# One request of weights moved up, one reciprocal moved ahead, one copy split over two engines: the start of an attention and GLU kernel on Trainium2

## The chip, the cores and the metric

The kernel runs on one core of one Trainium2 chip. The metric is the device time of one execution in microseconds (us). One execution was also recorded by the hardware profiler; all starts below are counted from the beginning of that record's span.

The engines are named as the profile names them: PE is TensorE (matmuls and transposes; PEld are its weight loads), DVE is VectorE, ACT is ScalarE, POOL is GpSimd, and SP is SyncE, which here only issues transfers.

## The reference

The input x has 2048 rows of 512 bf16 numbers. With `xn = layernorm(x)` over each row, the output is

```
q, k, v = split(xn @ wqkv)                 # 32 heads of 16
s = softmax(q . k[t - 2w], w = 0..7) v @ wo   # 8 keys, every second row back
g = silu((gelu(xn @ w_gate) * (xn @ w_up)) @ w_down)   # inner width 1792
out = x + s * g
```

So every projection needs the normalized rows first, with the 512 features on the partitions, that is, transposed.

## The kernel before

The rows are cut into 16 tiles of 128 (`NT`), and four tiles make one of four blocks (`TPQ` tiles, `TQ` = 512 rows, `NJ` blocks). For each block the kernel computes q, k and v (`qkv`), the gate and up projections (`glu`), the attention in pieces that are placed between those by a table written by hand (`at` and `run`, L426 to L468), and the down projection with the output (`down`, `finish`). The order of the program is the order on each engine: the schedule is manual (L51), and nothing reorders it later. Waits between engines are put in by the framework where one instruction reads or overwrites what another writes.

What the change touches is the start, up to the first 10 us, and it is all in the first block.

- **Loads** (L95 to L105). `load_x` (L84) fetches n tiles of x in one request, `load_w` (L90) a range of columns of a weight matrix. All are issued by SP, in the order written: x tiles 0, 1, 2, the q columns of `wqkv` (512 KB), x tile 3, the k columns, the v columns, x tiles 4 to 7, and then the gate and up weights and the other tiles.
- **Statistics of the first four tiles** (L171 to L180). `first_moments(t)` computes the row statistics (`bn_stats`, L172) and their aggregate (`bn_aggr`, L173) on VectorE, and the square root of the variance on ScalarE (L174). `first_normalize(t)` takes the reciprocal on VectorE (L179) and then normalizes (`normalize`, L194), which gives the tile `xn`.
- **Transposes** (L199 to L214). `transpose(t)` makes four 128 by 128 transposes on TensorE (L203) into one PSUM tile `tr`, and copies that into `xnT`, in one or in several parts; the copies run on ScalarE (L212), or on VectorE where `copy` is given (L214).
- **Warming matmuls** (`warm_up`, L216) on constants fill TensorE's time until the first tile is ready.
- **q, k and v of block 0** (L488 to L508). The first two tiles (`HQ` = 256 rows) are projected ahead of the other two. Their four q blocks go into one PSUM tile of four banks, `q4` (L488), in two rounds over the contraction. Each k block is one PSUM tile `qkv_ps` (L253), four matmuls (L238), and is drained to SBUF by ScalarE (L256 for q, L259 for k). Between them stand the transposes of tiles 2 and 3 (L495, L499), with their copies on VectorE. Then come the second 256 rows, and v.
- **PSUM.** Warming matmuls, transposes, projections and most outputs share the pool `mm` with four buffers (L71), which are given out in turn: a new tile takes the buffer of the tile four allocations earlier.

ScalarE's order in the start is: square roots of tiles 0 and 1, the copies of the transposes of tiles 0 and 1, square roots of tiles 2 and 3, four q drains, four k drains. VectorE's is: statistics and aggregate of tile 0, of tile 1, reciprocal and normalize of tile 0, of tile 1, statistics of tiles 2 and 3, their normalizes, the copies of their transposes.

Of the kernel before, what the change touches and what calls it, by code (L numbers as in the profile page):

```python
# [28 lines left out]
def kernel(  # L29
# [13 lines left out]
    nc = tc.nc  # L43
    B, S, D = A_x.shape
    DF = B_w_gate.shape[1]
    NT, NC, NF, NJ = S // P, D // P, DF // P, S // TQ
    TPQ = TQ // P
# [27 lines left out]
    x_sb = big.tile([P, NT, D], BF16, name="x_sb")  # L75
# [8 lines left out]
    def load_x(t, n=1):  # L84
        nc.sync.dma_start(
            out=x_sb[:, t : t + n, :],
            in_=x2d[t * P : (t + n) * P, :].rearrange("(t p) d -> p t d", p=P),
        )

    def load_w(dst, src, lo, hi):  # L90
        nc.sync.dma_start(
            out=dst[:, :, lo:hi], in_=src.rearrange("(k p) n -> p k n", p=P)[:, :, lo:hi]
        )

    for t in range(TPQ - 1):  # L95
        load_x(t)
    load_w(wqkv_sb, A_wqkv, 0, D)
    load_x(TPQ - 1)
    for i in range(1, 3):
        load_w(wqkv_sb, A_wqkv, i * D, (i + 1) * D)  # L100
    load_x(TPQ, TPQ)
# [5 lines left out]
    def load_late_weights():  # L107
# [16 lines left out]
        out=vT.rearrange("(k p) n -> p k n", p=P)[:, :, 0:PAD],  # L124
        in_=zpad[:],
# [32 lines left out]
    stats = const.tile([P, NT, nc.vector.BN_STATS_DIM], F32, name="stats")  # L158
# [9 lines left out]

    nc.scalar.activation(out=std[:, 0, :], in_=epsc[:], func=AF.Sqrt, bias=epsc[:], scale=1.0)

    def first_moments(t):  # L171
        nc.vector.bn_stats(out=stats[:, t, :], in_=x_sb[:, t, :])  # L172
        nc.vector.bn_aggr(out=mv[:, t, :], in_=stats[:, t, :])  # L173
        nc.scalar.activation(  # L174
            out=std[:, t, :], in_=mv[:, t, 1:2], func=AF.Sqrt, bias=epsc[:], scale=1.0
        )

    def first_normalize(t):
        nc.vector.reciprocal(out=rstd[:, t, :], in_=std[:, t, :])  # L179
        normalize(t)  # L180

    def moments(t):
        nc.vector.bn_stats(out=stats[:, t, :], in_=x_sb[:, t, :])
# [8 lines left out]
    def normalize(t):  # L192
        xn = xns[t] = xnp.tile([P, D], BF16, name="xn")
        nc.vector.tensor_scalar(  # L194
            out=xn[:], in0=x_sb[:, t, :], scalar1=mv[:, t, 0:1], scalar2=rstd[:, t, :],
            op0=ALU.subtract, op1=ALU.mult,
        )

    def transpose(t, parts=1, copy=None):  # L199
        xn = xns[t]  # L200
        tr = mm.tile([P, NC * P], BF16, name="tr", tag="mm")
        for c in range(NC):
            nc.tensor.transpose(tr[:, c * P : (c + 1) * P], xn[:, c * P : (c + 1) * P], ident[:])  # L203
        j, i = divmod(t, TPQ)
        if i == 0:
            xnT[j] = xtp.tile([P, NC, TQ], BF16, name="xnT")
        dst = xnT[j][:, :, i * P : (i + 1) * P]
        src = tr[:].rearrange("p (c n) -> p c n", c=NC)
        for k in range(parts):
            c = slice(k * NC // parts, (k + 1) * NC // parts)  # L210
            if copy is None:
                nc.scalar.activation(out=dst[:, c], in_=src[:, c], func=AF.Copy)  # L212
            else:
                copy(out=dst[:, c], in_=src[:, c])  # L214

    def warm_up(n, cols):  # L216

        ps = mm.tile([P, TQ], F32, name="warm_ps", tag="mm")
        for _ in range(n):
            nc.tensor.matmul(  # L220
                ps[:, 0:cols], lhsT=nc.const_aps.tensor(1.0, [P, P], BF16),
                rhs=nc.const_aps.tensor(1.0, [P, cols], BF16), start=True, stop=True,
            )
# [24 lines left out]
    def qkv(j, fo, i0=0, n=TQ, ps=None):  # L248
        which, c = divmod(fo, NC)
        if fo == 0 and i0 == 0:  # L250
            st[j]["q"] = qp.tile([P, NC, TQ], BF16, name="q_sb")
        if ps is None:
            ps = mm.tile([P, n], F32, name="qkv_ps", tag="mm")[:]  # L253
            project(ps, wqkv_sb, fo * P, j, i0, n)
        if which == 0:
            nc.scalar.activation(out=st[j]["q"][:, c, i0 : i0 + n], in_=ps, func=AF.Copy)  # L256
        elif which == 1:
            lo = PAD + j * TQ + i0
            nc.scalar.activation(out=k_sb[:, c, lo : lo + n], in_=ps, func=AF.Copy)  # L259
        else:  # L260
            vst = sm4.tile([P, TQ], BF16, name="vst")
            nc.scalar.activation(out=vst[:], in_=ps, func=AF.Copy)  # L262
            lo = PAD + j * TQ
            nc.sync.dma_start(out=vT[c * P : (c + 1) * P, lo : lo + TQ], in_=vst[:])
# [168 lines left out]
    for i in range(TPQ):  # L433
        at(("qkv", 0, i), normalize, TPQ + i)
        at(("glu", 0, 7 + i), moments, 2 * TPQ + i)
        if i < 2:
            at(("glu", 0, i), transpose, TPQ + i)
        at(("glu", 0, 8 + i), normalize, 2 * TPQ + i)
        at(("glu", 1, 0), transpose_by_dma, 2 * TPQ + i)
        at(("glu", 1, 10 + i), moments, 3 * TPQ + i)  # L440
        at(("qkv", 2, 2 * i), normalize, 3 * TPQ + i)
        at(("glu", 2, 0), transpose_by_dma, 3 * TPQ + i)
# [28 lines left out]
    HT = TPQ // 2  # L471
    HQ = HT * P
    warm_up(18, TQ // 2)
    warm_up(4, P)
    first_moments(0)
    first_moments(1)
    first_normalize(0)
    transpose(0)
    first_normalize(1)
    warm_up(4, P)  # L480
    transpose(1, parts=2)
    warm_up(4, P)
    first_moments(2)
    first_moments(3)
    first_normalize(2)
    first_normalize(3)

    q4 = att.tile([P, NC, TQ], F32, name="q4_ps", tag="quad")  # L488
    qs = [q4[:, fo, 0:HQ] for fo in range(NC)]
# [2 lines left out]
            project(qs[fo], wqkv_sb, fo * P, 0, 0, HQ, dks)  # L492
    for fo in range(NC):
        qkv(0, fo, 0, HQ, qs[fo])
    transpose(HT, copy=nc.vector.tensor_copy)  # L495
    for fo in range(NC, 2 * NC):
        qkv(0, fo, 0, HQ)
        if fo == NC:
            transpose(HT + 1, copy=nc.vector.tensor_copy)  # L499
    for t in range(TPQ, 2 * TPQ):  # L500
        moments(t)
    sum_constants()
# [61 lines left out]
```

The softmax here doesn't subtract the row's maximum and nothing guards it: scores larger than these inputs give would overflow.

## Time and profile before

| what | value |
|---|---|
| median of 4 runs | 229.87 us (229.72 to 230.38) |
| the profiled execution | 229.62 us |
| its span | 227.9 us |
| TensorE busy | 221.6 us, 97% |
| VectorE busy | 147.7 us, 65% |
| ScalarE busy | 129.7 us, 57% |
| granted TensorE clock | 1.00 |
| first q matmul | 6.64 us |
| DMA from 9.4 to 17.7 us | 369 GB/s |

The span is what the profiler recorded between the first and the last instruction; the device time is 1.7 us longer. A line of a timeline begins with the start and the length in us, then the engine, the line of the kernel and the operation, then output and inputs by name, their shapes, and how many such instructions were put together. The length of such a group reaches from the first start to the last end. In square brackets stands how long the engine had been idle, and who released it.

### The profile page before, as it was taken

The numbers are of one execution on the slowest core, as the hardware profiler recorded it, in microseconds if no ns is written. First come the engines' busy times: TensorE is split into PE (matmuls) and PEld (weight loads), VectorE is DVE, ScalarE is ACT, GpSimd is POOL, SyncE is SP. The second block draws the span as 40 slices with busy tenths as digits, with TensorE's granted clock in tenths as the row PEclk, the third lists the DMA queues.
The fourth block names the chain that finished last, engine by engine and source line by source line (L and its number), as shares of the span: only waits on it lengthen the run. The fifth ranks groups of instructions, "written<-read, shape, count | busy, mean of one in ns | idle before, by whom it ended". The sixth has DMA issues, their size and how long they took to land.

```text
span 227.9 us, 3495 instructions
## 1 busy us (share of the span) xinstructions
PE 221.6 (97%) x1300; PEld 106.1 (47%) x1320; DVE 147.7 (65%) x234; ACT 129.7 (57%) x213; POOL 12.8 (6%) x44
## 2 busy tenths in 40 slices
PE   7999999999999999999999999999999999999993
PEld 5864444444444444444444444444444444444453
DVE  4694996899596298865945369735476429943324
ACT  3779769764423876467621686746642387647210
POOL 1055023100000000110000000000000000000000
PEclk9999999999999999999999999999999999999999
DMA  5999589991399211110287511110139700001011
GB/s 164 361 371 373 142 165 198 214 238 42 97 196 211 65 27 26 26 29 0 92 168 168 140 30 23 26 36 5 40 106 213 175 26 3 0 6 26 0 45 48
DMA packets 31264, 24.62 MB, mean 108 GB/s; under 512 B 10896, under 2 KB 31248, under 8 KB 31248
## 3 DMA queue, kind: packets, MB, share of 16 engines
q1 hardware_dynamic: 31248, 24.41, 43.3%
q8 instruction: 10, 0.16, 0.3%
q14 instruction: 6, 0.05, 0.1%
HBM read 18.74 MB, written 4.34 MB: 101 GB/s over the span
## 4 chain that ended last, share of the span: by engine, by line
PE 93%; ACT 3%; DVE 1%; DMA 1%; issue 1%; ACTq 0%; DVEq 0%
PE u_ps L238 21%; PE y_ps L394 21%; PE g_ps L238 19%; PE qkv_ps L238 17%; PE s_ps L410 6%; PE L_ps L295 3%; PE o_ps L357 3%; DMA x_sb<-in_A_x_dram 1%; PE q_ps L238 1%; ACT u L384 1%; ACT xnT L212 1%; DVE stats L172 1%; ACT L382 1%; PE den_ps L315 0%; PE tr L203 0%
## 5 line engine op out<-in xcount | busy, mean ns | idle before, releaser
L238 PE MATMUL u_ps<-xnT,wu_sb 128*128 128x512 bf16 x224 | 57.5, 379 | 0.3
L238 PE MATMUL g_ps<-xnT,wg_sb 128*128 128x512 bf16 x213 | 56.3, 379 | 0.4
L394 PE MATMUL y_ps<-wd_sb,h 128*128 128x512 bf16 (+1 forms) x236 | 50.2, 366 | 0.1
L386 DVE TENSOR_TENSOR h<-ge,u 128x512 bf16<-128x512 bf16 x56 | 23.8, 424 | 37.6 <-ACT u L384 37.2
L284 DVE TENSOR_TENSOR pk<-q_sb,k_sb 128x2048 bf16<-128x2048 bf16 x32 | 37.5, 1218 | 7.0 <-ACT k_sb L259 7.0
L382 ACT ACTIVATE ge<-g_ps 128x512 bf16<-128x512 f32 x56 | 33.5, 598 | 14.9 <-PE g_ps L238 13.8
L384 ACT ACTIVATE u<-u_ps 128x512 bf16<-128x512 f32 x56 | 33.5, 598 | 14.7 <-PE u_ps L238 14.7
L238 PE MATMUL qkv_ps<-xnT,wqkv_sb 128*128 128x512 bf16 (+1 forms) x203 | 40.5, 354 | 0.3
L343 DVE TENSOR_TENSOR pv<-E,v_arr 128x2048 bf16<-128x2048 bf16 x32 | 38.7, 1220 | 0.7 <-PE u_ps L238 0.6
L394 PEld LDWEIGHTS <-h 128*128 128x128 bf16 x238 | 23.3, 98 | 25.3
L238 PEld LDWEIGHTS <-wu_sb 128*128 128x128 bf16 x224 | 21.9, 98 | 26.7 <-issue 0.3
L238 PEld LDWEIGHTS <-wg_sb 128*128 128x128 bf16 x224 | 21.2, 98 | 27.3 <-issue 3.0
L402 ACT ACTIVATE sl<-y_ps 128x512 bf16<-128x512 f32 (+1 forms) x17 | 9.7, 572 | 41.4 <-PE y_ps L394 39.0
L238 PEld LDWEIGHTS <-wqkv_sb 128*128 128x128 bf16 x224 | 21.8, 98 | 19.6 <-issue 0.2
L418 DVE TENSOR_TENSOR m<-s_ps,sl 128x512 bf16<-128x512 f32 (+1 forms) x17 | 11.2, 658 | 22.3 <-PE s_ps L410 22.3
L410 PE MATMUL s_ps<-wo_sb,oT 128*128 128x512 bf16 (+1 forms) x66 | 15.8, 366 | 0.2
L262 ACT ACTIVATE vst<-qkv_ps 128x512 bf16<-128x512 f32 x16 | 9.6, 597 | 6.7 <-PE qkv_ps L238 6.7
L188 POOL TENSOR_TENSOR rstd<-rstd,mhalf 128x1 f32<-128x1 f32 x12 | 7.7, 640 | 87.3 <-DVE rstd L185 87.3
L259 ACT ACTIVATE k_sb<-qkv_ps 128x512 bf16<-128x512 f32 (+1 forms) x20 | 10.2, 516 | 3.5 <-PE qkv_ps L238 3.2
L369 DVE TENSOR_TENSOR oT<-o_ps,rb 128x1024 bf16<-128x1024 f32 x8 | 9.4, 1218 | 2.5 <-DMA rb<-rs_d 2.5
L256 ACT ACTIVATE q_sb<-qkv_ps 128x512 bf16<-128x512 f32 (+1 forms) x16 | 8.7, 544 | 3.2 <-PE qkv_ps L238 3.0
L410 PEld LDWEIGHTS <-oT 128*128 128x128 bf16 x68 | 6.7, 98 | 7.2
(46 smaller groups left out, 104.0 us busy)
## 6 DMA issues: line engine op xcount, KB each, us to landing
v_arr<-vT SPq DMA_DIRECT2D x16, 520.0 KB, 5.5
vT<-vst SPq DMA_DIRECT2D x16, 128.0 KB, 1.9
out_dram<-o_t SPq DMA_DIRECT2D x15, 128.0 KB, 1.9
wg_sb<-in_B_w_gate_dram SPq DMA_DIRECT2D x2, 896.0 KB, 10.9
wu_sb<-in_B_w_up_dram SPq DMA_DIRECT2D x2, 896.0 KB, 12.9
wd_sb<-in_B_w_down_dram SPq DMA_DIRECT2D x1, 1792.0 KB, 12.5
wqkv_sb<-in_A_wqkv_dram SPq DMA_DIRECT2D x3, 512.0 KB, 5.0
x_sb<-in_A_x_dram SPq DMA_DIRECT2D x3, 512.0 KB, 11.9
```

Source lines behind the costliest of these rows:

```text
L238: nc.tensor.matmul(ps, lhsT=w[:, dk, lo : lo + P], rhs=xnT[j][:, dk, i0 : i0 + n], start=(dk == 0), stop=(dk == NC - 1),)
L259: nc.scalar.activation(out=k_sb[:, c, lo : lo + n], in_=ps, func=AF.Copy)
L262: nc.scalar.activation(out=vst[:], in_=ps, func=AF.Copy)
L284: nc.vector.tensor_tensor(out=pk[:], in0=st[j]["q"][:], in1=k_sb[:, :, off : off + TQ], op=ALU.mult)
L343: nc.vector.tensor_tensor(out=pv[:], in0=st[j]["E"][:, wh, :].unsqueeze(1).to_broadcast([P, 4, TQ]), in1=st[j]["va"][:, 4 * g : 4 * g + 4, ...
L382: nc.scalar.activation(out=ge[:], in_=g_ps[:], func=AF.Gelu_apprx_tanh)
L384: nc.scalar.activation(out=u[:], in_=u_ps[:], func=AF.Copy)
L386: nc.vector.tensor_tensor(out=h[:], in0=ge[:], in1=u[:], op=ALU.mult)
L394: nc.tensor.matmul(y[:], lhsT=st[j][fc][:, tt * P : (tt + 1) * P], rhs=wd_sb[:, fc, cols], start=(fc == 0), stop=(fc == NF - 1),)
L402: nc.scalar.activation(out=sl[:], in_=y[:], func=AF.Silu)
L410: nc.tensor.matmul(s[:], lhsT=st[j]["oT"][:, g, tt * P : (tt + 1) * P], rhs=wo_sb[:, g, cols], start=(g == 0), stop=(g == NC - 1),)
L418: nc.vector.tensor_tensor(out=m[:], in0=s[:], in1=sl[:], op=ALU.mult)
```

## The change

It has four parts, all in the start.

1. The request for the q columns of `wqkv` goes from behind x tile 2 to behind x tile 1; x tiles 2 and 3 follow it together.
2. The pieces of `first_moments` and `first_normalize` are cut anew into `first_stats`, `first_moments` and `first_rstd`, so that tile 0's reciprocal stands between tile 1's statistics and tile 1's aggregate on VectorE. For tiles 2 and 3 the order stays as it was: statistics and aggregate of one and of the other, then reciprocal and normalize of each.
3. Of the two halves of the copy of tile 1's transpose, the first goes to VectorE and the second stays on ScalarE. On VectorE it stands ahead of the statistics of tile 2.
4. The transposes of tiles 2 and 3 go from ahead of the first and the second k block to behind the first and the second k block.

```diff
-    for t in range(TPQ - 1):
-        load_x(t)
+    load_x(0)
+    load_x(1)
     load_w(wqkv_sb, A_wqkv, 0, D)
-    load_x(TPQ - 1)
+    load_x(2)
+    load_x(3)
...
+    def first_stats(t):
+        nc.vector.bn_stats(out=stats[:, t, :], in_=x_sb[:, t, :])
+
     def first_moments(t):
-        nc.vector.bn_stats(out=stats[:, t, :], in_=x_sb[:, t, :])
         nc.vector.bn_aggr(out=mv[:, t, :], in_=stats[:, t, :])
...
-    def first_normalize(t):
+    def first_rstd(t):
         nc.vector.reciprocal(out=rstd[:, t, :], in_=std[:, t, :])
-        normalize(t)
...
-            if copy is None:
+            if copy is None or k % 2:
                 nc.scalar.activation(out=dst[:, c], in_=src[:, c], func=AF.Copy)
...
+    first_stats(0)
     first_moments(0)
+    first_stats(1)
+    first_rstd(0)
     first_moments(1)
-    first_normalize(0)
+    normalize(0)
     transpose(0)
-    first_normalize(1)
+    first_rstd(1)
+    normalize(1)
     warm_up(4, P)
-    transpose(1, parts=2)
+    transpose(1, parts=2, copy=nc.vector.tensor_copy)
     warm_up(4, P)
-    first_moments(2)
-    first_moments(3)
-    first_normalize(2)
-    first_normalize(3)
+    for t in (2, 3):
+        first_stats(t)
+        first_moments(t)
+    for t in (2, 3):
+        first_rstd(t)
+        normalize(t)
...
-    transpose(HT, copy=nc.vector.tensor_copy)
     for fo in range(NC, 2 * NC):
         qkv(0, fo, 0, HQ)
-        if fo == NC:
-            transpose(HT + 1, copy=nc.vector.tensor_copy)
+        if fo < NC + 2:
+            transpose(HT + fo - NC, copy=nc.vector.tensor_copy)
```

## The prediction

> **What bounds the kernel now.** I read four views in this order: the page, the busy time by stretches, the timelines of VectorE and ScalarE over the start, and that of TensorE. The page first:
>
> ```profile
> PE 221.6 (97%) x1300; PEld 106.1 (47%) x1320; DVE 147.7 (65%) x234; ACT 129.7 (57%) x213; POOL 12.8 (6%) x44
> PE 93%; ACT 3%; DVE 1%; DMA 1%; issue 1%; ACTq 0%; DVEq 0%
> ```
>
> TensorE is busy for 97% of the span and holds 93% of the chain that ended last, at a granted clock of 1.00. From 20.8 to 220 us it is busy 198.2 of 199.2 us (the stretches), and it computes the same list of matmuls after the change. So the change can only move time in the start: whatever TensorE begins earlier or later there is carried to the end, plus any new gap. The start runs on VectorE and ScalarE until about 6.6 us:
>
> ```profile
> 4.51 0.18 DVE L173 BATCH_NORM_AGGREGATE mv<-stats 128x2 f32<-128x6 f32 x1
> 4.61 0.13 DVE L179 RECIPROCAL rstd<-std 128x1 f32<-128x1 f32 x1
> 4.78 0.41 DVE L194 TENSOR_SCALAR xn<-x_sb,mv,rstd 128x512 bf16<-128x512 bf16 x1
> 5.11 0.16 DVE L179 RECIPROCAL rstd<-std 128x1 f32<-128x1 f32 x1
> 5.30 0.41 DVE L194 TENSOR_SCALAR xn<-x_sb,mv,rstd 128x512 bf16<-128x512 bf16 x1
> 5.63 0.69 DVE L172 BATCH_NORM_STATS2 stats<-x_sb 128x6 f32<-128x512 bf16 x1
> ...
> 6.77 0.69 DVE L172 BATCH_NORM_STATS2 stats<-x_sb 128x6 f32<-128x512 bf16 x1 [0.24 <-DMA x_sb<-in_A_x_dram]
> ```
>
> Tile 0's reciprocal starts 0.10 us behind tile 1's aggregate; its input, the square root on ScalarE, was there at 4.29 (4.00 + 0.29). Tile 2's statistics start at 5.63, tile 3's wait for their data until 6.77. Then the first real matmuls, and who drains them:
>
> ```profile
> 5.77 0.40 PE L203 MATMUL tr<-ident,xn 128*128 128x128 bf16 x4
> 6.01 0.39 PE L220 MATMUL warm_ps<-const-bfloat16-1.0 128*128 128x128 bf16 x4
> 6.64 1.91 PE L238 MATMUL q_ps<-xnT,wqkv_sb 128*128 128x256 bf16 x16 [0.24 <-ACT xnT L212]
> 8.39 0.39 PE L203 MATMUL tr<-ident,xn 128*128 128x128 bf16 x4
> 8.61 0.60 PE L238 MATMUL qkv_ps<-xnT,wqkv_sb 128*128 128x256 bf16 x4
> 9.05 0.39 PE L203 MATMUL tr<-ident,xn 128*128 128x128 bf16 x4
> ...
> 8.59 1.21 ACT L256 ACTIVATE q_sb<-q_ps 128x256 bf16<-128x256 f32 x4 [0.58 <-PE q_ps L238]
> 9.66 1.50 ACT L259 ACTIVATE k_sb<-qkv_ps 128x256 bf16<-128x256 f32 x4
> ```
>
> The first q matmul, at 6.64, waits for ScalarE's copy of the first half of tile 1's transpose (that copy starts at 6.21 and ends near 6.60). ScalarE begins to drain q at 8.59, only when the last of the 16 q matmuls has ended (6.64 + 1.91 = 8.55), and drains the first k block from 9.66 to 10.07. TensorE's and ScalarE's timelines at 20 us show a rule of this kernel's PSUM pool of four buffers that decides the case:
>
> ```profile
> 20.12 0.60 ACT L382 ACTIVATE ge<-g_ps 128x512 bf16<-128x512 f32 x1
> 20.77 1.02 PE L238 MATMUL u_ps<-xnT,wu_sb 128*128 128x512 bf16 x4
> ```
>
> The allocations run tr, g, u, tr, g, u here; the second u is the fifth after the first g, takes its buffer, and starts 0.05 us after that g was drained (20.12 + 0.60 = 20.72). So a block waits until the block four allocations before it is drained.
>
> [...]the trace has 0.42 for that copy (8.81 and 9.47). [...]landings follow issues: q 6.4, x tile 3 6.74, k 8.2, v 9.8 us.
>
> **The change part by part.**
>
> *Requests.* q's weights are issued third instead of fourth: at about 1.70 instead of 2.18, as the x requests before it take 0.39 to 0.43 us of SP's queue each. Between 3.6 and 4.6 us the DMA engines moved only 92 to 195 GB/s, so the half megabyte starts into a gap: it lands about 0.48 us earlier, near 5.9. Tile 2 now stands behind it. A tile is 0.35 us (128 KB at about 370 GB/s). All together starts 0.48 earlier and tile 2's 0.35 comes behind, so k lands 0.13 earlier, near 8.1, tile 3 near 6.6, tile 2 near 6.26; at worst, with no gain from the gap, tile 2 lands 0.35 ahead of today's tile 3, at 6.39. SP's later requests keep place and time. On the path q's weights are worth nothing, since ScalarE's copy (6.60) ended after their landing (6.4); but without the earlier landing an earlier copy would be worth little.
>
> *Reciprocal ahead of the aggregate.* Tile 1's statistics run from 3.82 to 4.48. The reciprocal goes at about 4.40 (instructions without a wait start some 0.08 us before the end of the one before: 5.63 against 5.71), the aggregate stays at 4.51, and the normalize follows at 4.61 instead of 4.78: 0.17 us for tile 0. Tile 1 gets less. Its square root still starts at 4.73 and ends at 5.03, so its reciprocal starts at 5.07 instead of 5.11, its normalize at 5.26 instead of 5.30, its transpose ends at 6.13 instead of 6.17. Gain on the path: **0.04 us**. Tile 0's 0.17 is hidden behind that; its copy on ScalarE (0.60) ends at 6.11, in time.
>
> *Half of the copy on VectorE.* [...]Bounds: 0.21 (half of 0.42) and 0.42 (no saving). I take 0.29: a gain of **0.10 us**, from 0.21 down to a loss of 0.03. The copy runs 6.17 to 6.46 and q starts at 6.50 instead of 6.64. ScalarE's half follows at 6.50 and ends at 6.88; the ninth matmul needs it at 6.50 + 8 x 0.109 = 7.37, so it costs nothing while it is under 0.5 us late. Queued behind the copy on VectorE is tile 2's work: its statistics go from 5.63 to about 6.40, 0.77 us later. By today's spacings (0.72 to the aggregate, 0.10 to the next statistics, 0.72 to the next aggregate) tile 3's aggregate ends near 8.12, its square root on ScalarE at 8.45, tiles 2 and 3 are normalized at 8.6 and 9.15.
>
> *Transposes moved behind k blocks 0 and 1.* Left in place, tile 2's transpose would now wait some 0.4 us (wanted at 8.25, ready at 8.66). Moved, it is wanted at 8.25 + 4 x 0.108 = 8.68 and tile 3's at 9.33: no wait of note. The k weights are wanted 0.25 us earlier on TensorE than today (8.25 less 0.1 for the load), about when they land.
>
> But the order of PSUM allocations changes with it. Before: tile 2, k0, tile 3, k1, k2, k3; k2 takes the buffer of tile 2's transpose, drained at 9.23, and k3 that of k0. After: k0, tile 2, k1, tile 3, k2, k3; **k2 takes k0's buffer**. ScalarE drains k0 behind four q drains, which start at the end of the last q matmul: 6.50 + 1.91 + 0.04 = 8.45, plus 1.07 (9.66 - 8.59) = 9.52, plus 0.41 = 9.93. So k2 starts at 9.97. TensorE arrives there at 9.33 + 0.22 = 9.55 and stands for 0.42 us. Before, k2 started at 9.71 (tile 3's transpose at 9.05, 0.22 for it, 0.44 for k1), and k3 found k0 drained at 10.07, just ahead of 10.14. The next blocks find their buffers drained (k1's at 10.2, wanted at 10.84).
>
> The sum: q earlier by 0.04 + 0.10 = 0.14; k2 later by 9.97 - 9.71 = **0.26 us**, which is the same as a new wait of 0.40 against today's order less 0.14. From there TensorE runs on without a gap to 17.5 us, and the stall of 20.12 to 20.77 follows the last v block's drain on ScalarE, so it shifts along. Gate and up weights land at 13.7 and 17.5, no later than now. The profiled execution took 229.62 us (span 227.9 and 1.7 around it): 229.88 after. The median of the four runs is 229.87, 0.25 above it, so 230.13 there, 0.11% slower.
>
> **The rivals.** *No stall at k2*: the buffer is free, or ScalarE starts q's drains as each block ends, as early as 7.9. For it: nothing in the code makes the first drain wait for the last matmul. Against: 8.59 is what the trace shows, and u at 20.77. Then 0.14 us of gain stays, 229.73; with the copy at its best 0.3, 229.6. *Slower by more than can be measured*: ScalarE's FIFO holds tile 3's square root ahead of q's drains, and I have them tied, 8.45 both. Should tile 2 land only at today's 6.74, the statistics start at 6.78, the root ends at 8.83, q's drains start at about 8.75 and k2 at 10.27: 0.56 us later, 230.43. It decides from drains starting at 8.65, thus from tile 2 landing at about 6.64. Against it: the order of landings. *Hidden altogether*: q's gain and the stall nearly cancel, 0.11 us, 229.98, if VectorE takes only 0.21 for its copy and starts after two of four transposes (6.06).
>
> **How the numbers follow.** About 0.2% (0.46 us) is what a measurement can tell from no change, and the four runs span 0.66. The stall as worked out: 0.64, nearly all of it within 0.2%, its own range 229.9 to 230.35; the nearly cancelled form 0.10; no stall 0.12; the late square root 0.14. Slower by over 0.2%: most of the last, and the tail of the first that scatter puts there, 0.19. Faster: a part of no stall, by scatter, 0.05. The rest, 0.76, is the same. The range, 229.55 to 230.6, takes in the ends of the copy and both outer rivals with scatter.
>
> **What would show it.** The q matmuls at about 6.50; VectorE's half copy of 0.29 us; tile 2's statistics near 6.40; q's drains from 8.45; k2's first matmul about 9.97, named as waiting for ScalarE's k drain or as a plain gap of 0.4 us ahead of it; the v blocks some 0.26 us later than now. Wrong if k2 follows tile 3's transpose without a gap, if q's drains start behind the square root, or if a new gap stands after 10 us.

## The result

The changed kernel takes 1.0029 times the time of the kernel before (95% interval 1.0021 to 1.0036): medians of 230.52 and 230.00 us. It is slower by about 0.3%, some 0.5 to 0.7 us, where the prediction had 0.11% and put the time within what a measurement can tell from no change. The ratio is taken over executions in the fast state (without one of the changed kernel at 233.50 us and one of the kernel before at 296.23 us), so it is not the quotient of the medians, which is 1.0023. The time lies in the predicted range by luck: the cause is not the predicted one.

The page of the changed kernel has the same list of work, but for the half copy that went from ScalarE to VectorE. In its chain of work that ended last a transfer now holds 3%, and VectorE nothing:

```profile
PE 222.9 (98%) x1300; PEld 107.0 (47%) x1320; DVE 147.7 (65%) x235; ACT 129.7 (57%) x212; POOL 12.8 (6%) x44
PE 92%; DMA 3%; ACT 2%; SPq 1%; issue 1%; DVE 0%; ACTq 0%; DVEq 0%
```

The chain in order of time over the start names the transfer (start and length in us, then what the end of the kernel waited for). It is the request for the k columns, issued at 3.21 and landed at 9.16, straight ahead of the first k block:

```profile
3.21 5.95 DMA wqkv_sb<-in_A_wqkv_dram
9.16 0.05 issue
9.21 0.61 PE qkv_ps L240 x4
9.81 0.22 PE tr L205 x4
```

TensorE's timeline of the changed kernel shows two differences from the kernel before, and only the second belongs to the change:

```profile
5.05 0.63 PE L205 MATMUL tr<-ident,xn 128*128 128x128 bf16 x4
...
5.91 0.63 PE L205 MATMUL tr<-ident,xn 128*128 128x128 bf16 x4
...
7.01 1.91 PE L240 MATMUL q_ps<-xnT,wqkv_sb 128*128 128x256 bf16 x16
9.21 0.61 PE L240 MATMUL qkv_ps<-xnT,wqkv_sb 128*128 128x256 bf16 x4 [0.28 <-DMA wqkv_sb<-in_A_wqkv_dram]
...
10.55 7.98 PE L240 MATMUL qkv_ps<-xnT,wqkv_sb 128*128 128x256 bf16 x55
```

First, the transposes take 0.63 us instead of 0.40 and q starts at 7.01, 0.37 later than before (6.64). That is TensorE's rate, and chance, as the runs below show. Second, k0 starts at 9.21. TensorE was free for it at 7.01 + 1.75 = 8.76 (in the kernel before, q's 16 matmuls held it from 6.64 to 8.39), so it stands still for 0.45 us; the 0.28 in the bracket counts from the modelled end of the last q matmul. k2 follows at 10.55 instead of 9.71: 0.37 + 0.45 + 0.02 = 0.84 us. The drain of the last v block is 0.84 later too (18.57 against 17.73), and of that 0.75 is left near the end (the chain's last product on VectorE at 225.34 against 224.59).

VectorE's timeline of the changed kernel has the order that was meant, nearly on the predicted times up to the half copy, which follows the late transposes:

```profile
4.39 0.14 DVE L182 RECIPROCAL rstd<-std 128x1 f32<-128x1 f32 x1
4.51 0.18 DVE L176 BATCH_NORM_AGGREGATE mv<-stats 128x2 f32<-128x6 f32 x1
4.61 0.38 DVE L196 TENSOR_SCALAR xn<-x_sb,mv,rstd 128x512 bf16<-128x512 bf16 x1
5.05 0.16 DVE L182 RECIPROCAL rstd<-std 128x1 f32<-128x1 f32 x1
5.25 0.41 DVE L196 TENSOR_SCALAR xn<-x_sb,mv,rstd 128x512 bf16<-128x512 bf16 x1
6.58 0.29 DVE L216 COPY xnT<-tr 128x256 bf16<-128x256 bf16 x1 [0.91 <-PE tr L205]
6.78 0.69 DVE L173 BATCH_NORM_STATS2 stats<-x_sb 128x6 f32<-128x512 bf16 x1
```

### The profile page after: what moved, and what is told of

Its sections match the earlier page's. It is cut to its first block, busy times and chain, and to the rows that moved or that the text cites. A ratio compares the mean times of both kernels' runs of the same rounds, so it can differ in the third digit from the quotient of the medians.

```text
span 228.6 us, 3496 instructions
## 1 busy us (share of the span) xinstructions
PE 222.9 (98%) x1300; PEld 107.0 (47%) x1320; DVE 147.7 (65%) x235; ACT 129.7 (57%) x212; POOL 12.8 (6%) x44
## 4 chain that ended last, share of the span: by engine, by line
PE 92%; DMA 3%; ACT 2%; SPq 1%; issue 1%; DVE 0%; ACTq 0%; DVEq 0%
PE u_ps L240 21%; PE y_ps L396 21%; PE g_ps L240 19%; PE qkv_ps L240 17%; PE s_ps L412 6%; PE L_ps L297 3%; PE o_ps L359 3%; DMA wqkv_sb<-in_A_wqkv_dram 3%; ACT u L386 1%; SPq L85 1%; ACT L384 1%; PE den_ps L317 0%; ACT ge L384 0%; ACT vst L264 0%; ACT xnT L214 0%
```

## The experiments

Three theories stood after the result. **Late k**: the new order of requests makes the k columns land later, and k0 waits. **PSUM**: the prediction's step, k2 waits for the drain of k0. **Chance of one execution**: what the profile shows differently does not belong to the change.

### The whole, and its two halves

`after_again` is the changed kernel once more.

> The changed kernel once more, to see what of its first profile repeats. Order of requests (the k weights land late because of the new order): the k weights land near 9.2 us again and TensorE waits some 0.4 us for them ahead of the first k block; ratio to before 1.003. PSUM buffer (the third k block waits for the drain of the first): k weights near 8.1, the wait ahead of the third k block, ratio 1.001. Chance of one execution: a first q matmul near 6.5 if TensorE reaches full rate before the first transposes, near 7.0 if not.

`requests_only` is the kernel before with the new order of requests alone:

```diff
-    for t in range(TPQ - 1):
-        load_x(t)
+    load_x(0)
+    load_x(1)
     load_w(wqkv_sb, A_wqkv, 0, D)
-    load_x(TPQ - 1)
+    load_x(2)
+    load_x(3)
```

> The kernel before with the new order of requests alone. Order of requests: k weights near 9.2, TensorE waits about 0.5 us for them at the first k block (wanted at 8.61), ratio 1.002 or more. PSUM buffer: no change in what TensorE waits for, since its allocations are as before; ratio 1.000, k weights near 8.1.

`rest_only` is the changed kernel with that edit taken back.

> The changed kernel with the requests in the old order. Order of requests: the k weights land at 8.2 as before, nothing is lost, ratio 0.9995 to 1.000. PSUM buffer: the third k block waits 0.3 to 0.4 us for the drain of the first, ratio 1.001 (0.26 us).

Measured against the kernel before, on one chip: `after_again` 1.0021 (1.0011 to 1.0031), `requests_only` 1.0025 (1.0015 to 1.0034), `rest_only` 1.0005 (0.9993 to 1.0018). The order of the requests alone costs as much as the whole change; the other three parts together cost and bring nothing that can be told. (In the profile of `rest_only` q starts at 6.73, behind its own columns, which landed at 6.68; so the run does not give those parts a clear path.) TensorE's timeline of `after_again`, then of `requests_only`:

```profile
5.83 0.38 PE L205 MATMUL tr<-ident,xn 128*128 128x128 bf16 x4
...
6.69 1.91 PE L240 MATMUL q_ps<-xnT,wqkv_sb 128*128 128x256 bf16 x16 [0.25 <-DVE xnT L216]
9.38 0.61 PE L240 MATMUL qkv_ps<-xnT,wqkv_sb 128*128 128x256 bf16 x4 [0.79 <-DMA wqkv_sb<-in_A_wqkv_dram]
```

```profile
6.59 1.91 PE L239 MATMUL q_ps<-xnT,wqkv_sb 128*128 128x256 bf16 x16 [0.24 <-ACT xnT L213]
8.60 0.40 PE L204 MATMUL tr<-ident,xn 128*128 128x128 bf16 x4
9.20 0.61 PE L239 MATMUL qkv_ps<-xnT,wqkv_sb 128*128 128x256 bf16 x4 [0.19 <-DMA wqkv_sb<-in_A_wqkv_dram]
```

Both wait for the k columns at the first k block, which landed at 9.3 and 9.15. In `after_again` q begins at 6.69 instead of 7.01, with the second transpose back at 0.38 us: the late q of the first profile does not repeat, the wait for k does. TensorE was free for k0 at 6.69 + 1.75 = 8.44 and stands still for 0.94 us, which is 0.49 longer than in the first profile: 0.32 that q gained and 0.17 by which k0 is later. In `requests_only` a second wait is mixed in: tile 2 lands later in the new order, so its transpose, which stands ahead of k0 there, starts at 8.60 and not at 6.59 + 1.75 = 8.34. The k columns still come last (8.60 + 0.22 = 8.82, against 9.15), but this run alone does not price them; `k_from_q_weights` below does.

`rest_only` also decides on PSUM. ScalarE's drain of k0 and TensorE's first k2 matmul there, as two narrow windows of the timelines show them:

```profile
9.76 0.42 ACT L260 ACTIVATE k_sb<-qkv_ps 128x256 bf16<-128x256 f32 x1
...
9.97 0.27 PE L239 MATMUL qkv_ps<-xnT,wqkv_sb 128*128 128x256 bf16 x1
```

k0 is drained at 9.76 + 0.42 = 10.18; k2 starts at 9.97, straight behind tile 3's transpose (9.73 + 0.22 = 9.95). So k2 does not use k0's buffer. In the trace its first matmul waits for a semaphore of VectorE and for none of ScalarE. Which buffer it takes stays open. The statement that a new tile takes the buffer of the tile four allocations earlier, made in the description of the kernel and in the prediction, doesn't hold here.

`k0_on_vector` tests the same from the other side:

```diff
-            nc.scalar.activation(out=k_sb[:, c, lo : lo + n], in_=ps, func=AF.Copy)
+            if j == 0 and fo == NC and i0 == 0:
+                nc.vector.tensor_copy(out=k_sb[:, c, lo : lo + n], in_=ps)
+            else:
+                nc.scalar.activation(out=k_sb[:, c, lo : lo + n], in_=ps, func=AF.Copy)
```

> The changed kernel with the first k block drained by VectorE, which takes the four q drains from ahead of that drain. Order of requests: no change against the changed kernel, ratio to before 1.003, k weights near 9.2. PSUM buffer: the wait ahead of the third k block is gone, 0.4 us less than the changed kernel, ratio 0.9995 to 1.001.

Measured: 1.0045 (1.0027 to 1.0062). Nothing is gained, as late k has it; whether the drain on VectorE costs something of its own these intervals do not say. In its profile k landed at 8.9.

### What the k columns are worth

`k_from_q_weights` takes the wait away by other data: in the changed kernel, the k blocks of the first 256 rows are multiplied with q's columns, which have landed. k is therefore not the reference's k there.

```diff
-            project(ps, wqkv_sb, fo * P, j, i0, n)
+            early = j == 0 and i0 == 0 and which == 1
+            project(ps, wqkv_sb, (c if early else fo) * P, j, i0, n)
```

> The changed kernel, in which the k blocks of the first 256 rows are multiplied with q's weights instead of k's (so k is not computed as the reference has it there), so that they do not wait for the k request. If the late k weights are the whole loss: q, k0, the transpose of tile 2 and k1 follow without a wait, ratio to before 0.999 to 1.0005. If the loss is somewhere else in the changed start (later tiles, VectorE's order, the PSUM pool): 1.002 or more.

Measured: 1.0006 (0.9996 to 1.0016), with TensorE's timeline:

```profile
0.84 3.84 PE L222 MATMUL warm_ps<-const-bfloat16-1.0 128*128 128x256 bf16 x22 [0.84 <-PEq L556]
5.07 0.40 PE L205 MATMUL tr<-ident,xn 128*128 128x128 bf16 x4 [0.39 <-DVE xn L196]
...
6.61 1.91 PE L240 MATMUL q_ps<-xnT,wqkv_sb 128*128 128x256 bf16 x16 [0.24 <-DVE xnT L216]
8.36 0.60 PE L240 MATMUL qkv_ps<-xnT,wqkv_sb 128*128 128x256 bf16 x4
...
9.70 2.56 PE L240 MATMUL qkv_ps<-xnT,wqkv_sb 128*128 128x256 bf16 x22
```

The loss is gone with the wait: the interval does not meet that of the changed kernel (1.0021 to 1.0036). This is also the plain view of what the other parts bring when nothing is in their way: q at 6.61 and k2 at 9.70, against 6.64 and 9.71 before. That is no gain that can be told from scatter, as `requests_only`, with the old chain, had q at 6.59. k2 again has no gap in front of it.

`after_k_halves` leaves the mathematics alone and asks for the k columns in two requests, of which the first is enough for k0 and k1:

```diff
-    for i in range(1, 3):
-        load_w(wqkv_sb, A_wqkv, i * D, (i + 1) * D)
+    for lo, hi in ((D, D + D // 2), (D + D // 2, 2 * D), (2 * D, 3 * D)):
+        load_w(wqkv_sb, A_wqkv, lo, hi)
```

> The changed kernel with the k columns in two requests of 256 KB. The first half is enough for k0 and k1. Late k weights as the cause: the first half lands about 0.7 us sooner than the whole, near 8.4, the wait ahead of k0 is 0.2 us or less and the ratio about 1.000 to 1.0015. If three short requests in a row spread the rings further, the first half lands at 9 again and the ratio stays at 1.003.

Measured: 0.9995 (0.9987 to 1.0004). The first half landed at 7.8, and TensorE's timeline has no wait ahead of k0:

```profile
6.55 1.91 PE L240 MATMUL q_ps<-xnT,wqkv_sb 128*128 128x256 bf16 x16 [0.25 <-DVE xnT L216]
8.29 0.60 PE L240 MATMUL qkv_ps<-xnT,wqkv_sb 128*128 128x256 bf16 x4
8.80 0.40 PE L205 MATMUL tr<-ident,xn 128*128 128x128 bf16 x4
```

So the change with this repair is as fast as the kernel before, and not measurably faster. None of the versions in these runs is.

### Chance: the kernel before against itself

> The kernel before against itself: ratio 1.000. Its profile shows whether the first transposes can also take 0.63 us there instead of 0.40, with the first q matmul near 7.0 instead of 6.64: if so, that difference between the two first profiles is chance and not the change. The k weights should land at 8.2 to 8.7.

Measured: 0.9988 (0.9974 to 1.0002), which also says how far two measurements of one kernel can lie apart. TensorE's timeline:

```profile
0.84 4.42 PE L220 MATMUL warm_ps<-const-bfloat16-1.0 128*128 128x256 bf16 x22 [0.84 <-PEq L548]
5.27 0.61 PE L203 MATMUL tr<-ident,xn 128*128 128x128 bf16 x4
...
6.99 1.91 PE L238 MATMUL q_ps<-xnT,wqkv_sb 128*128 128x256 bf16 x16 [0.24 <-ACT xnT L212]
```

The unchanged kernel has the slow transposes and the late q too. Its 22 warming matmuls took 4.42 us, as in the changed kernel's first profile, against 3.68 in the first profile of before and 3.84 in `k_from_q_weights`: TensorE went over to its faster rate at a different moment. In the first profile of before one warming matmul of 256 columns follows the other by 0.21 us up to 3.56 and by 0.11 us from then on, 2.7 us after the first of them at 0.83. In the changed kernel's first profile the matmuls keep the slow distance until 6.6 (0.11 us for 128 columns, against 0.06 later). The row of the granted clock reads 1.00 in all four and does not show it. What sets the moment is not shown. Against expectation, k landed at 9.0 here and not by 8.7: the unchanged order can have a late k too.

### Why k lands later

The last runs ask what in the order does it. `x23_one`, `q_behind_x3`, `x3_behind_k` and `q_delayed` start from `requests_only` and change the head of the list of requests:

```diff
     load_x(0)
     load_x(1)
     load_w(wqkv_sb, A_wqkv, 0, D)
-    load_x(2)
-    load_x(3)
+    load_x(2, 2)
```

> The kernel before with the new order of requests, x tiles 2 and 3 in one request of 256 KB. Two theories on why the k weights land about 1 us later in the new order. Small requests: two short requests in a row ahead of k's make the transfer engines run dry or apart; with one request k lands near 8.2, ratio 1.000. Early q: the big q request issued at 1.71 instead of 2.18, while the first tiles are still under way, drives the rings apart, whatever follows; k lands near 9.1 again, ratio 1.0025.

```diff
-    load_x(0)
-    load_x(1)
-    load_w(wqkv_sb, A_wqkv, 0, D)
-    load_x(2)
-    load_x(3)
+    for t in range(TPQ):
+        load_x(t)
+    load_w(wqkv_sb, A_wqkv, 0, D)
```

> The kernel before with q's weights behind x tile 3, so that no tile stands between q and k and q is issued at about 2.7. Early q: k lands near 8.2 on all rings, as before or sooner; q lands near 6.75, so the first q matmul is 0.1 to 0.2 us later than 6.64; ratio 1.0005. Small requests: the same, k lands near 8.2. If k lands near 9 here too, both are wrong and only the order of before is good.

```diff
     load_x(2)
+    load_w(wqkv_sb, A_wqkv, D, 2 * D)
     load_x(3)
-    for i in range(1, 3):
-        load_w(wqkv_sb, A_wqkv, i * D, (i + 1) * D)
+    load_w(wqkv_sb, A_wqkv, 2 * D, 3 * D)
```

> The kernel before with the order x0, x1, q, x2, k, x3, v: q early, and one tile between q and k, as many bytes and requests ahead of k as two tiles less one. Small requests: k lands 0.35 us ahead of 8.2, near 7.8. Early q: k lands near 8.8 or later (9.15 less 0.35). Tile 3 lands behind k in both, so that its statistics and transpose are late by 1.4 us or more, and the time says little: ratio 1.002 to 1.006.

```diff
     load_x(1)
+    spare = const.tile([16, D], BF16, name="spare")
+    nc.sync.dma_start(out=spare[:], in_=x2d[0:16, :])
     load_w(wqkv_sb, A_wqkv, 0, D)
```

> The kernel before with the new order of requests and one request of 16 KB ahead of q's, to no tile that is used, so that q is issued near 2.15 as in the kernel before and all later requests some 0.45 us later than in the new order. Early q: k lands on all rings together, near 8.3 to 8.6; ratio 1.001. Small requests: k lands at 9.2 to 9.6; ratio 1.003 or more.

`after_x23` is the changed kernel with `load_x(2, 2)` in place of the two requests.

> The changed kernel with x tiles 2 and 3 in one request. Late k weights as the cause: k lands near 8.15 on all rings and is not waited for; tile 2 lands at 6.7 instead of 6.3, so its transpose is ready at about 8.95 and is waited for some 0.25 us behind k0; ratio 1.000 to 1.001. If the loss is not the k weights: 1.002 or more as in the changed kernel.

The trace has sixteen completions for each request; where the expectations speak of rings, these are what was measured. The table gives when the k request's first, eighth or ninth, and last completion came (us from the span's start). k0 waits for the last: it starts at 9.21, 9.38 and 9.20 in `after`, `after_again` and `requests_only`, 0.04 to 0.05 behind it.

| kernel | directly ahead of k | first | middle | last | ratio to before |
|---|---|---|---|---|---|
| before | q, one tile | 7.5 | 8.1 | 8.3 | 1 |
| before_again | q, one tile | 7.8 | 8.0 | 9.0 | 0.9988 (0.9974 to 1.0002) |
| rest_only | q, one tile | 7.7 | 8.0 | 8.6 | 1.0005 (0.9993 to 1.0018) |
| after | q, two tiles | 7.9 | 8.2 | 9.2 | 1.0029 (1.0021 to 1.0036) |
| after_again | q, two tiles | 7.4 | 8.0 | 9.3 | 1.0021 (1.0011 to 1.0031) |
| requests_only | q, two tiles | 7.5 | 8.0 | 9.15 | 1.0025 (1.0015 to 1.0034) |
| k0_on_vector | q, two tiles | 7.3 | 8.0 | 8.9 | 1.0045 (1.0027 to 1.0062) |
| k_from_q_weights | q, two tiles | 7.6 | 8.0 | 8.7 | 1.0006 (0.9996 to 1.0016) |
| after_k_halves, first half | q, two tiles | 6.9 | 7.4 | 7.8 | 0.9995 (0.9987 to 1.0004) |
| x23_one | q, two tiles in one | 7.8 | 7.9 | 8.2 | 1.0018 (1.0012 to 1.0025) |
| after_x23 | q, two tiles in one | 7.7 | 8.0 | 8.75 | 1.0001 (0.9993 to 1.0009) |
| x3_behind_k | q, one tile | 7.2 | 7.5 | 7.95 | 1.0044 (1.0032 to 1.0056) |
| q_delayed | q, two tiles (0.46 later) | 7.8 | 8.45 | 9.7 | 1.0084 (1.0054 to 1.0114) |
| q_behind_x3 | q, behind four tiles | 7.95 | 8.1 | 9.45 | 1.0009 (1.0000 to 1.0018) |

The middle completion comes at 8.0 to 8.2 in either order, about as predicted. What moves is the last: 8.3, 8.6 and 9.0 with the order of before (the first three rows), mean 8.6; 8.7 to 9.3 in the five rows with q early and two tiles behind it, mean 9.05. The two sets overlap, so one profile of each would not prove it. The ratios of `requests_only`, `k_from_q_weights` and `after_k_halves`, which rest on many executions, show that the order costs time and that the cost goes with the wait for k. In `after_again` fifteen completions have come by 8.2 and a single one comes at 9.34.

Three of the four orders speak for short requests in a row ahead of a long one, and against q's early issue: with q early but two tiles in one request, or one tile, k's completions stay within 0.4 and 0.8 us of each other; with q as late as before but two tiles behind it (and one short request more ahead of it), they lie 1.9 us apart. The order of the first of them gave a wider spread in `after_x23`, 1.1 us. The fourth, `q_behind_x3`, answers as neither theory had it: no tile stands between q and k, yet k landed at 9.45, where both had 8.2. Four tiles stand directly ahead of q there, and q's own completions were 1.5 us apart, as k's were then. TensorE's timeline shows it by the wait:

```profile
8.05 1.92 PE L237 MATMUL q_ps<-xnT,wqkv_sb 128*128 128x256 bf16 x16 [1.44 <-DMA wqkv_sb<-in_A_wqkv_dram]
```

Both theories had expected q to land at 6.75; it landed at 8.00. The ratio of 1.0009 (1.0000 to 1.0018) says that such a wait is not the rule in it: the profiled execution, 231.13 us, was the slowest of 22. Each order was profiled once, and `before_again` shows how much that can mislead: that short requests in a row widen the spread is what these profiles suggest, not settled. What the traces do show are single slow packets. In their lists of DMA packets, most of them of 1 KB, the median between 6 and 9 us is 0.046 to 0.049 us (0.032 in `after_k_halves`, whose two k requests have packets of half that size). Beside these stand a few packets of over 0.2 us: in all seven profiles with two single tiles behind q (from one in `after_again`, of 0.55, to fourteen in `q_delayed`), in `before_again` (seven) and in `q_behind_x3` (eight). In the first profile of before and in `rest_only`, `x23_one`, `after_x23` and `x3_behind_k` there is none. The lists do not say which completion a packet belongs to, so that these packets hold up the late completions is not shown, and why they take so long stays open.

Three ratios of this group are not about k alone. In `x23_one` k came in time (8.2), yet the time is 1.0018. Both tiles land together at 6.7, so tile 2's statistics start at 6.69, where `requests_only` had them at 6.35 and the kernel before at 5.63; tile 2 is then normalized at 8.88 (8.47 + 0.41), and its transpose, ahead of k0 in this order, would be wanted at 8.39 by a q that starts at 6.64. That these 0.5 us are the loss is argued, not tested by itself. `after_x23`, where the transpose stands behind k0, is at 1.0001, though in its one profile (230.41 us, the third slowest of 13) k landed at 8.75, not at the expected 8.15, and k0 waited. In `x3_behind_k` tile 3 lands behind k and its chain holds TensorE for 1.08 us. In `q_delayed` the loss of 0.84%, some 1.9 us, is more than the one wait of its profile, 9.78 against 8.61 before at k0; the profiled execution, 230.89 us, was the second fastest of eight, and where the rest goes is not shown.

## Why the prediction was wrong

The prediction's sum had one loss, a wait for PSUM at k2, and one gain, an earlier q. That loss is not in the traces, of the gain at most a part is, and the loss that was measured stood in the sum at nothing. By its own steps:

- **Requests.** Landings of q (5.9 predicted, 6.0 measured), tile 2 (6.26, 6.35) and tile 3 (6.6, 6.7) were right. "k lands 0.13 earlier, near 8.1" was the step that failed: 9.2 in the first profile, 8.7 to 9.3 in five. Bytes over bandwidth give the middle completion, 8.0 to 8.2, and k0 waited for the last. That the sixteen keep step was the author's assumption: k's came from 7.54 to 8.26 before, and from 7.92 to 9.16 in the changed kernel's first profile.
- **The wait it made.** The prediction saw that k is wanted 0.25 us earlier "about when they land" and priced that at nothing. With no slack, any lateness counts in full: 0.45 us in the first profile, 0.94 in the second. This term, the loss of the changed kernel, was missing from the sum and from the rivals.
- **PSUM.** The 0.40 us wait at k2, and with it the predicted 0.26, does not exist. k2 follows tile 3's transpose without a gap (10.55 against 10.31 + 0.22 = 10.53), which the prediction had named as a sign that it is wrong. That is its first rival's case, but that rival's 0.14 us of gain is not there either. The observation it came from was one block: u at 20.77, 0.05 behind the drain of g, which is the fourth allocation before it and not the fifth. The order of the buffers at k2 was inferred from that. The sign of the sum came out right for a wrong reason.
- **Reciprocal and copy.** Right on their own engines: 4.39, 4.51, 4.61, 5.05 and 5.25 against 4.40, 4.51, 4.61, 5.07 and 5.26, and 0.29 us for VectorE's half copy. The predicted 0.29 was the author's estimate between two bounds, 0.42 and its half: in the kernel before, VectorE took 0.42 us for each copy of 512 elements (8.81 and 9.47, tiles 2 and 3), and ScalarE 0.38 for each of its two half copies of tile 1. That ScalarE's half follows VectorE's was also an estimate, and the trace has it so: it starts at 6.90, behind 6.58 + 0.29, and waits for VectorE's copy by the profile.
- **From the copy to q.** The prediction started q 0.04 us behind the end of VectorE's copy, as it stands behind ScalarE's in the kernel before. Measured are 0.14 to 0.15 us in all five profiles with the split copy in which q's columns had landed by then, against 0.05 in the six without it that do not wait for those columns. So the 0.10 us that the copy saves is lost again. The first q matmul now needs copies of two engines. In the kernel before, TensorE loaded its weights at 6.41, ahead of the copy's end (6.21 + 0.38 = 6.59). With the split copy the traces have one more instruction on TensorE's queue, a wait for VectorE's semaphore (6.91 to 6.96 in the changed kernel's first profile), and the weight load stands behind it: at 6.98 there, and at 6.58 in `k_from_q_weights`, where the copy ended at 6.18 + 0.29 = 6.47. Weight loads (PEld) of the kernel before, then VectorE's copy and the weight loads of `k_from_q_weights`:

```profile
6.41 0.98 PEld L238 LDWEIGHTS <-wqkv_sb 128*128 128x128 bf16 x8 [0.19 <-DMA wqkv_sb<-in_A_wqkv_dram]
```

```profile
6.18 0.29 DVE L216 COPY xnT<-tr 128x256 bf16<-128x256 bf16 x1 [0.49 <-PE tr L205]
6.58 0.89 PEld L240 LDWEIGHTS <-wqkv_sb 128*128 128x128 bf16 x9 [0.39 <-issue]
```

Of the predicted gain of 0.14 us at q, the 0.04 of the reciprocal is left, and scatter covers it: q started at 6.55 to 6.61 in the profiles of `k_from_q_weights`, `after_k_halves` and `after_x23`, against 6.64 before, 6.59 in `requests_only` and 6.50 predicted. That the second wait is what delays q is read from the traces; no run takes it away by itself.

- **Transposes.** Tile 2's wait behind k0 was small, as said: 0.07 us in `after_k_halves` (8.80 against 8.29 + 0.44), none in `k_from_q_weights`. Where tiles 2 and 3 landed late, at 7.25 in `after_x23`, it was 0.29 (9.53 against 8.80 + 0.44).
- **The slower rival** named q's drains behind tile 3's square root: not seen in the changed kernel. In `after_again` the root ended at 8.48 (8.19 + 0.29) and the drains started at 8.64, behind the last q matmul. In `after_x23` the drains did stand behind the root (they start at 9.22, with the root from 9.01 to 9.31 and the last q matmul done at 8.48), and k2 still had no gap (10.45 against 10.20 + 0.22).

## What to carry to other kernels

Each request has sixteen completions here, and k0 started 0.04 to 0.05 us behind the last of them (at 9.20 to 9.38), where the middle one had come at 8.0 to 8.2: when a change makes the reader of a transfer ready earlier, ask for the landing's spread over several profiles, not for bytes over bandwidth. A part that brings 0.1 us is worth nothing where the next wait is for a transfer whose landing varies: by 0.8 us here between two profiles of the kernel before (8.26 and 9.02). Before a copy is divided between two engines, read what its reader waits for: here the reader waited for both, and started 0.1 us later behind the copy. A long request of which the first reader needs half can be cut in two, which here took the loss of 0.3% away (0.9995, 0.9987 to 1.0004).

## What the runs showed of the hardware

- The first and the last of one request's sixteen completions came 0.4 us apart (k in `x23_one`) up to 1.9 us apart (k in `after_again` and `q_delayed`). In the changed kernel's first profile, where k landed 0.90 us later than before (9.16 against 8.26), the requests issued behind it were as late: v and x tiles 4 to 7 landed at 10.65 and 12.15, against 9.76 and 11.26.
- The moment at which TensorE's matmuls began to follow each other at the shorter distance (0.11 us for 256 columns instead of 0.21) varied from one execution to the next: 3.6 us in the first profile of the kernel before, and 6.1 in the second, where four transposes took 0.61 us until then and 0.42 from there. The first q matmul stands at 6.64 and 6.99 there, with the granted clock at 1.00 throughout.
- Between 6 and 9 us single DMA packets took up to 1.17 us (`q_behind_x3`), with a median of 0.046.
- The first q matmul started 0.14 to 0.15 us behind the end of VectorE's half copy where two engines shared the copy, and 0.05 behind ScalarE's where one made it.
